# Queues that give each engine one piece of side work per half step in a four-layer attention and Fourier kernel

## The chip, the cores and the metric

The kernel runs on one core of one Trainium2 chip. The time is device microseconds of one launch, and the figure that counts is the median of several runs: 2229.14 us before the change (three runs: 2230.31, 2229.14 and 2216.46). The engines are TensorE (PE in the profile, PEld for its weight loads), VectorE (DVE), ScalarE (ACT), GpSimd (POOL) and SyncE (SP), which issues the transfers of this kernel in order.

## The reference

Four layers on an `x` of 2048 rows and 640 columns, all in float32: causal attention in a window of 256 rows with 32 heads of 20 columns, a Fourier mixing by matrices, and the same two again.

```python
def _A_ref(x, wqkv, wo):
    qkv = (x @ wqkv).reshape(B, S, 3, H, Dh).transpose(2, 0, 3, 1, 4)
    q, k, v = qkv[0], qkv[1], qkv[2]
    scores = einsum("bhqd,bhkd->bhqk", q, k) * (Dh ** -0.5)
    scores = where(0 <= i - j < 256, scores, -1e9)
    p = softmax(scores, axis=-1)
    return einsum("bhqk,bhkd->bhqd", p, v).transpose(0, 2, 1, 3).reshape(B, S, D) @ wo

def _B_ref(x, dft_seq_re, dft_seq_im, dft_hid_re, dft_hid_im):
    a = einsum("bsd,ed->bse", x, dft_hid_re)
    b = einsum("bsd,ed->bse", x, dft_hid_im)
    return einsum("ts,bse->bte", dft_seq_re, a) - einsum("ts,bse->bte", dft_seq_im, b)

x = x + _A_ref(_layernorm(x), A_wqkv, A_wo)
x = x + _B_ref(_layernorm(x), dft_seq_re, dft_seq_im, dft_hid_re, dft_hid_im)
x = x + _A_ref(_layernorm(x), A_wqkv, A_wo)
x = x + _B_ref(_layernorm(x), dft_seq_re, dft_seq_im, dft_hid_re, dft_hid_im)
```

## The kernel before

**Split operands.** Every large operand of a product is kept as two tiles: a leading part, which is the value rounded to the matmul's fp32r format, and a remainder, which is the value less its leading part. A product is three matmuls (leading by leading, leading by remainder, remainder by leading). So a tile that is to be multiplied is *cut*: one instruction writes the leading part (ACT, L180 in `split`, or a cast on POOL, L498) and one subtracts it from the value (L186 in `split`, on DVE or POOL, or L499 on POOL).

**The heads.** This is the middle part of each attention layer, and the change is almost all in it. The 32 heads are taken in 8 quads of 4, a quad in 16 steps of 128 rows: steps t = 0 to 127, 10 lead steps ahead of them, and two half steps (z = 0 and 1, two heads each) in each step. In a half step:

- PE makes the transposed scores of two heads for step t (`t_pair`, L595), the scores of two heads for step t + 10, of which only the row maxima are wanted (`s_head`, L567), and in the second half step the product of the probabilities with the values for step t - 1 (`pv`, L630, 24 matmuls).
- DVE adds the mask to each score tile and takes its row maximum (L572, two in a half step, each followed by a short read of the maximum). The bank is free when that is done.
- ACT takes the exponential (L605) and copies the product out (L637).
- POOL sets the probabilities outside the window to zero (L611 and L615, one pair in a half step). `pv` of a step needs them.

The three stages share a ring of six banks. A transposed score tile takes a bank that an L572 of the half step before has freed, so an L572 that is late makes the next half step's PE work late; masks that are late make `pv` late.

**Side work.** In the first half step PE also has a *fill*: matmuls of other work, taken in order from `more()`. In quads 0 to 5 these are the projections of later quads (`pieces`, L211, 64 rows by 512 columns). When a piece is complete its result is copied out by ACT (L497), cast by POOL one half step later (L498), subtracted by POOL one later (L499), and stored to memory four later (L500 and on, `store_qk`). Of its three buffers named `c`, the next piece but two takes the same one. The projection weights are cut as they come (`cut_chunk`, L186 on POOL, 384 and 256 columns). From t = 95 the fill is the output projection of the first three of five pieces of the heads' results, 16 tiles of 128 rows (`partials`); a tile is two fills of 18 matmuls of 320 columns, and DVE adds its two halves to `x` (L899). The remaining two pieces come after the heads (`late`).

**What a partial needs.** `load_o` loads a piece of the heads' results and the reciprocals of its row sums, multiplies them on POOL (L816, 8 half steps after the loads) and cuts the product (L186, POOL, 10 after). The output weights are cut too (`prepare`, L186, 640 columns on POOL; `poll_late`, L186 on DVE, in the same half step as the ACT part). `load_o` waits until its row sums are stored: it runs `tick` in a loop, and everything that is due in the skipped half steps is issued there and then. A row sum is loaded two half steps after its heads are done, its reciprocal (L650, DVE) is issued seven half steps after, and its store nine after (`finish`).

**Order.** `post(d, f)` runs `f` d half steps later; `tick` ends a half step and runs all that is due. Nothing limits how much one engine gets in a half step.

## Time and profile before

| what | us |
|---|---|
| median of three runs | 2229.14 |
| the profiled execution, its own time | 2223.97 |
| its span in the trace | 2222.2 |
| heads of the first attention layer, quads 0 to 7 | 161.72 to 543.98 |
| heads of the second attention layer | 1266.02 to 1644.50 |

The profile page gives for each group of instructions a line number, an engine, an operation and its tiles, then its busy time and the mean of one in ns, and the idle time just before it with what ended most of it. The window rows give the start and end of a stretch, its length, each engine's busy time with its number of instructions in brackets (PE, PEld, DVE, ACT, POOL), the clock that TensorE was granted (1.00 is full), the DMA share and GB/s. In a timeline row the first figure is the start, the second the length, and a bracket at its end says how long the engine had been idle and what ended that.

### The profile page before, as it was taken

To read this page: it belongs to the slowest core of one execution; us is meant where nothing else is said; L and a number is where in the kernel's file an instruction comes from. 1 tells how busy PE (TensorE), PEld (TensorE's weight loads), DVE (VectorE), ACT (ScalarE), POOL (GpSimd) and SP (SyncE) were. 2 spreads that over 40 slices of the span, in tenths; PEclk is the share of its full clock that TensorE was granted. 3 is DMA by queue.
4 is the path that set the end of the run, shared out by engine and by line. 5 is a ranking of instruction groups with operands and counts; after the bars stand their busy time and mean duration, and the time that the engine had idled before them with its cause. 6 is when DMAs were issued, how large, how long until landed. Compare 5 with 4: busy or idle time off the path is not lost.

```text
span 2222.2 us, 48837 instructions
## 1 busy us (share of the span) xinstructions
PE 2130.6 (96%) x17944; PEld 1782.5 (80%) x17944; DVE 1603.5 (72%) x3947; ACT 1128.9 (51%) x2101; POOL 1004.8 (45%) x1534
## 2 busy tenths in 40 slices
PE   7999999989989999999999999999989999999999
PEld 7887777677768888889999777776777688888899
DVE  6347788775897868785661578887758978687776
ACT  3116776656554545452441277776555545455432
POOL 3027777766614222332330476768665132332324
PEclk9999999999999999999999999999999999999999
DMA  5546656774535354656646466668754354546653
GB/s 184 171 148 187 195 182 204 221 205 142 181 125 184 120 183 141 211 182 199 209 145 185 153 184 192 192 200 232 201 168 148 118 186 142 170 138 220 218 163 129
DMA packets 220175, 392.10 MB, mean 176 GB/s; under 512 B 39200, under 2 KB 85792, under 8 KB 219936
## 3 DMA queue, kind: packets, MB, share of 16 engines
q1 hardware_dynamic: 219936, 388.98, 55.7%
q8 instruction: 142, 2.33, 0.4%
q14 instruction: 97, 0.79, 0.1%
HBM read 273.94 MB, written 113.77 MB: 174 GB/s over the span
## 4 chain that ended last, share of the span: by engine, by line
PE 71%; POOL 8%; DVE 8%; DMA 4%; issue 4%; ACT 4%; SPq 1%; POOLq 0%; ACTq 0%; DVEq 0%
PE banks L1280 27%; PE banks L193 14%; PE banks L211 10%; PE banks L630 6%; PE banks L1568 5%; PE banks L595 4%; PE banks L567 4%; POOL pt L611 2%; POOL pt L615 1%; POOL c L499 1%; POOL big L186 1%; ACT pt L605 1%; DVE qp L186 1%; DVE banks L572 1%; DMA vq<-v_d 1%
## 5 line engine op out<-in xcount | busy, mean ns | idle before, releaser
L572 DVE CUSTOM_DVE_ANT_0 banks<-banks,mask 128x384 f32<-128x384 f32 (+2 forms) x1024 | 528.0, 557 | 150.5 <-PE banks L567 127.9
L605 ACT ACTIVATE pt<-banks 128x768 f32<-128x768 f32 (+2 forms) x512 | 394.5, 772 | 165.8 <-PE banks L595 75.7
L611 POOL TENSOR_SCALAR_AFFINE_SELECT pt<-pt 128x256 f32<-128x256 f32 x512 | 210.5, 412 | 205.3 <-ACT pt L605 187.1
L211 PE MATMUL banks<-big,wc 64*128 64x512 f32 x1920 | 269.8, 395 | 0.4 <-DVE pt L396 0.4
L630 PE MATMUL banks<-pt,vq 128*32 128x128 f32 x5760 | 218.9, 279 | 12.1 <-POOL pt L611 12.1
L595 PE MATMUL banks<-qp,kp 61*128 61x384 f32 (+2 forms) x1024 | 208.2, 382 | 17.0 <-DVE mc L572 12.3
L567 PE MATMUL banks<-kp,qp 60*128 60x384 f32 (+2 forms) x1024 | 201.5, 347 | 12.9 <-DVE mc L572 10.8
L186 DVE TENSOR_TENSOR qp<-pt,qp 128x512 fp32r<-128x512 f32 (+1 forms) x209 | 178.7, 858 | 38.8 <-ACT qp L180 37.6
L211 PEld LDWEIGHTS banks<-big,wc 64*128 64x128 f32 x1920 | 185.1, 186 | 24.3 <-ACT x L497 1.8
L630 PEld LDWEIGHTS banks<-pt,vq 128*32 128x32 f32 x5760 | 145.0, 110 | 64.6 <-issue 37.0
L180 ACT ACTIVATE qp<-pt 128x512 fp32r<-128x512 f32 (+1 forms) x209 | 129.1, 624 | 118.6 <-DVE pt L1214 54.7
L615 POOL TENSOR_SCALAR_AFFINE_SELECT pt<-pt 128x256 f32<-128x256 f32 x448 | 184.6, 412 | 0.0
L595 PEld LDWEIGHTS banks<-qp,kp 61*128 61x128 f32 x1024 | 106.9, 186 | 81.2 <-DVE mc L572 52.0
L1280 PE MATMUL banks<-qp,big 128*128 128x512 f32 x630 | 153.4, 394 | 6.6 <-POOL big L186 3.9
L1213 POOL TENSOR_TENSOR pt<-pt,pt 128x512 f32<-128x512 f32 x34 | 50.6, 1489 | 240.3 <-DMA pt<-c 133.7
L567 PEld LDWEIGHTS banks<-kp,qp 60*128 60x128 f32 x1024 | 122.2, 188 | 36.7 <-DVE mc L572 22.5
L572 DVE DVE_READ_ACCUMULATOR2_ANT mc<- 128x1 f32 x1024 | 145.5, 142 | 0.0
L1280 PEld LDWEIGHTS banks<-qp,big 128*128 128x128 f32 x630 | 118.0, 189 | 32.9 <-POOL big L186 5.4
L180 ACT ACTIVATE c<-pt 128x512 fp32r<-128x512 f32 x144 | 88.2, 625 | 86.9 <-DVE pt L1214 41.1
L1280 PE MATMUL banks<-qp,xc 128*128 128x512 f32 x480 | 119.0, 391 | 6.8 <-DVE xc L186 4.2
L637 ACT ACTIVATE ou<-banks 128x128 f32<-128x128 f32 x256 | 71.5, 279 | 87.4 <-PE banks L630 76.7
L186 DVE TENSOR_TENSOR c<-pt,c 128x512 fp32r<-128x512 f32 x140 | 109.7, 789 | 8.4 <-ACT c L180 5.9
(241 smaller groups left out, 4469.8 us busy)
## 6 DMA issues: line engine op xcount, KB each, us to landing
pt<-c SPq DMA_DIRECT2D x188, 512.0 KB
qk_d<-c SPq DMA_DIRECT2D x80, 512.0 KB
kp<-qk_d SPq DMA_DIRECT2D x384, 80.0 KB
qp<-qk_d SPq DMA_DIRECT2D x384, 80.0 KB
kp<-u_d SPq DMA_DIRECT2D x32, 640.0 KB
o_d<-ou SPq DMA_DIRECT2D x64, 256.0 KB
x_d<-x SPq DMA_DIRECT2D x48, 320.0 KB
v_d<-pt SPq DMA_DIRECT2D x16, 768.0 KB
```

Of the source, the lines that this page charges most:

```text
L180: nc.scalar.activation(hi, src, AF.Copy, scale=-1.0 if neg else 1.0)
L186: (eng or nc.vector).tensor_tensor(out=lo, in0=src, in1=hi.bitcast(F32), op=OP.subtract)
L193: self.nc.tensor.matmul(p, x, y, start=n == 0, stop=n == last)
L211: self.nc.tensor.matmul(ps[a], x[r], y[r], start=half + i == 0, stop=half == 1 and i == n - 1, skip_group_check=True)
L567: nc.tensor.matmul(p, qp[quad % 2][b:b + 60, z, qb * P:(qb + 1) * P], kp[quad % 2][b:b + 60, z, k0 * P:(qb + 1) * P], start=True, stop=True)
L572: nc.vector.tensor_tensor_reduce(out=p, in0=p, in1=self.mask[:, 384 - n * P:], scale=1.0, scalar=NEG, op0=OP.add, op1=OP.max, accum_out=mc ...
L595: nc.tensor.matmul(self.banks[:, banks[e], :n * P], kp[quad % 2][b:b + 61, z, kb * P:(kb + 1) * P], qp[quad % 2][b:b + 61, z, kb * P:(kb + ...
L605: nc.scalar.activation(pt[quad, kb][:, 2 * z:2 * z + 2, :n * P], self.banks[:, b0:b1 + 1, :n * P], AF.Exp, scale=SCALE)
L611: nc.gpsimd.affine_select(out=t[:, :, 0:P], in_=t[:, :, 0:P], pattern=[[0, 2], [1, P]], compare_op=OP.is_ge, fill=0.0, base=0, channel_mul ...
L615: nc.gpsimd.affine_select(out=t[:, :, 256:384], in_=t[:, :, 256:384], pattern=[[0, 2], [-1, P]], compare_op=OP.is_gt, fill=0.0, base=0, ch ...
L630: nc.tensor.matmul(self.banks[32 * h:32 * h + 32, bank, :P], vq[:, 96 * (kb % 4) + 21 * h:96 * (kb % 4) + 21 * h + 32], t[:, h, (qb - kb) ...
L1280: nc.tensor.matmul(self.banks[:, bk, :], p, b[q], start=start and m == 0, stop=stop and last and m == 2, skip_group_check=True)
```

## The change

The change gives each of ACT, DVE and POOL a queue of pieces (`lanes`). `tick` still runs all that was posted, and then takes at most one piece from each queue. `job` puts a piece in a queue, `sub_job` a subtraction (in two halves if it is for POOL), `cut_job` a leading part for ACT which, when it runs, puts the subtraction in another queue; `flush` issues what is left under a name at once, and stands ahead of the uses.

- In `pieces` the cast stays on POOL; its subtraction goes to DVE half a step later, the store two after that.
- The weight cuts in `cut_chunk`, in `prepare` and in `poll_late` take ACT for the leading part and DVE, half a step later, for the remainder.
- `load_o` no longer waits by running `tick`; it posts itself again for the next half step. Its multiplication is two halves of 256 columns on POOL, one per half step. The cut's remainder is on POOL for the first piece, on DVE for the others.
- The reciprocal is issued 9 half steps after its heads are done, its store 11, and the store counts as done 2 half steps later.
- `more()` gives out no partial whose pieces aren't ready; a partial's sum is one addition of 640 columns (L970 of the new kernel) in place of two of 320.
- `pack`, which moves a quad's projected rows, waits for the stores of its rows.
- Two conditions more hold back steps of the Fourier layer that would overtake the late pieces, and a list of places there is in another order.

```diff
     def tick(self):
         self.slot += 1
         for k in sorted(k for k in self.posted if k <= self.slot):
             for f in self.posted.pop(k):
                 f()
+        for lane in self.lanes.values():
+            if lane and lane[0][0] <= self.slot:
+                lane.popleft()[2]()
+
+    def job(self, lane, key, fn):
+        if self.slot is None or self.after:
+            fn()
+        else:
+            self.lanes[lane].append((self.slot + 1, key, fn))
...
+    def sub_job(self, lane, key, lo, src, hi, done=None):
+        eng = {"dve": self.nc.vector, "pool": self.nc.gpsimd}[lane]
+        n = 2 if lane == "pool" else 1
+        w = src.shape[-1] // n
+        for i in range(n):
+            c = slice(i * w, (i + 1) * w)
+            def sub(c=c, last=i == n - 1):
+                eng.tensor_tensor(out=lo[..., c], in0=src[..., c], in1=hi[..., c].bitcast(F32), op=OP.subtract)
+                if last and done:
+                    done()
+            self.job(lane, key, sub)
+
+    def cut_job(self, lane, key, hi, lo, src, done=None):
+        def first():
+            self.nc.scalar.activation(hi, src, AF.Copy)
+            self.sub_job(lane, key, lo, src, hi, done)
+        self.job("act", key, first)
...
-            for i, ks in enumerate((slice(0, 3), slice(3, KC))):
-                self.post(3 * i, lambda ks=ks: self.split(w[:, 0, ks], w[:, 1, ks], raw[:, ks], eng=self.nc.gpsimd))
+            for ks in (slice(0, 3), slice(3, KC)):
+                self.cut_job("dve", ("w", c), w[:, 0, ks], w[:, 1, ks], raw[:, ks])
...
             self.nc.scalar.activation(r, p, AF.Copy)
-            self.post(1, lambda: self.nc.gpsimd.tensor_copy(st[:, 0, :], r))
-            self.post(2, lambda: self.nc.gpsimd.tensor_tensor(
-                out=st[:, 1, :], in0=r, in1=st[:, 0, :].bitcast(F32), op=OP.subtract))
-            self.post(6, lambda: self.store_qk(c, sb, st))
+            def cast():
+                self.nc.gpsimd.tensor_copy(st[:, 0, :], r)
+                self.sub_job("dve", ("qk", c, sb), st[:, 1, :], r, st[:, 0, :],
+                             lambda: self.post(2, store))
...
+            self.job("pool", ("qk", c, sb), cast)
...
-            at = (2, 7, 9) if quad < NQ - 1 else (1, 5, 6)
+            at = (2, 9, 11) if quad < NQ - 1 else (1, 5, 6)
...
-                self.stored.add((quad, bk))
+                self.post(2 if quad < NQ - 1 else 0, lambda: self.stored.add((quad, bk)))
...
-            if not made[0] and self.early_o[0]["left"]:
+            if not self.left and not self.ready_part():
                 return None
...
+        if not self.after and not all((q, sb) in self.stored for q in range(h0 // 4, h1 // 4)):
+            def again():
+                o["left"] -= 1
+                self.load_o(o, sb, k, raw, rr)
+            self.post(1, again)
+            return
...
-        self.post(8, lambda: nc.gpsimd.tensor_tensor(out=raw, in0=raw, in1=rr, op=OP.mult))
-        self.post(10, cut)
+        def parts():
+            hi, lo = o[k]
+            self.cut_job("pool" if k == 0 else "dve", key, hi, lo, raw, lambda: self.post(0 if k < EARLY else 3, done))
+        def half(i):
+            cs = slice(i * 256, (i + 1) * 256)
+            nc.gpsimd.tensor_tensor(out=raw[:, cs], in0=raw[:, cs], in1=rr[:, cs], op=OP.mult)
+            if i:
+                parts()
+        for i in range(2):
+            self.post(7, lambda i=i: self.job("pool", key, lambda: half(i)))
...
-            next(self.early_l[2])
-            for i in range(2):
-                self.defer(2 + 2 * i, lambda i=i: next(self.early_l[i]))
+            for k in (2, 0, 1):
+                self.cut_job("dve", "ew", *self.early_w[k], self.early_raw[k])
...
-            for hf in range(2):
-                cs = slice(hf * 320, (hf + 1) * 320)
-                nc.vector.tensor_tensor(out=y[:, cs], in0=ps[hf], in1=y[:, cs], op=OP.add)
+            nc.vector.tensor_tensor(out=y, in0=self.banks[:, b0:b0 + 2, :320], in1=y, op=OP.add)
...
-            self.split(hi[:, cs], lo[:, cs], r[:, cs])
+            self.cut_job("dve", "lw", hi[:, cs], lo[:, cs], r[:, cs])
...
+        if any(n >= at and (len(self.late_o) <= sb or self.late_o[sb]["left"]) for sb, at in ((2, 4), (3, 7))):
+            return False
```

On POOL in quad 0, at steps 3 to 5, stood these rows before; `c` is a projected piece, `wc` a weight, `pt_94` to `pt_97` are the probabilities of four successive steps.

```order
L498 CAST c<-x 128x512
L611 AFFINE_SELECT pt_97<-pt_97 128x2x128
L615 AFFINE_SELECT pt_97<-pt_97 128x2x128
L499 TENSOR_TENSOR c<-x,c 128x512
L498 CAST c<-x 128x512
L611 AFFINE_SELECT pt_94<-pt_94 128x2x128
L615 AFFINE_SELECT pt_94<-pt_94 128x2x128
L186 TENSOR_TENSOR wc<-x,wc 128x384
L499 TENSOR_TENSOR c<-x,c 128x512
L611 AFFINE_SELECT pt_94<-pt_94 128x2x128
L615 AFFINE_SELECT pt_94<-pt_94 128x2x128
```

At the same place stand now:

```order
L543 CAST c<-x 128x512
L666 AFFINE_SELECT pt_97<-pt_97 128x2x128
L670 AFFINE_SELECT pt_97<-pt_97 128x2x128
L543 CAST c<-x 128x512
L666 AFFINE_SELECT pt_94<-pt_94 128x2x128
L670 AFFINE_SELECT pt_94<-pt_94 128x2x128
L666 AFFINE_SELECT pt_94<-pt_94 128x2x128
L670 AFFINE_SELECT pt_94<-pt_94 128x2x128
```

All subtractions have left this stretch; two casts are all that is left between the masks (L666 and L670 are the old L611 and L615).

On DVE in quad 1, at steps 3 and 4, stood nothing before but mask additions (`ISA banks,mc<-banks,mask`) with their reads, and a reciprocal ahead of these steps.

```order
L572 ISA banks,mc<-banks,mask 128x384
L572 ISA mc 128x1
L572 ISA banks,mc<-banks,mask 128x384
L572 ISA mc 128x1
L650 RECIPROCAL rc<-sm 128x16
L572 ISA banks,mc<-banks,mask 128x384
L572 ISA mc 128x1
```

There stand now, one or two between each pair of mask additions (L627 is the old L572, L207 the new subtraction):

```order
L207 TENSOR_TENSOR c<-x,c 128x512
L627 ISA banks,mc<-banks,mask 128x384
L627 ISA mc 128x1
L627 ISA banks,mc<-banks,mask 128x384
L627 ISA mc 128x1
L207 TENSOR_TENSOR c<-x,c 128x512
L627 ISA banks,mc<-banks,mask 128x384
L627 ISA mc 128x1
L627 ISA banks,mc<-banks,mask 128x384
L627 ISA mc 128x1
L705 RECIPROCAL rc<-sm 128x16
L207 TENSOR_TENSOR wc<-x,wc 128x384
```

The subtraction of the other 256 columns of `wc` follows behind the next pair. The four subtractions of this stretch come in four half steps on end, and two more of `c` come at steps 11 and 12 of the same quad.

On PE at the first partial, the end of quad 5, stood before (L630 is `pv`, L211 with `big` tiles the partial):

```order
L630 MATMUL banks<-pt_97,vq_92 32x128 x4
L630 MATMUL banks<-pt_94,vq_93 32x128 x4
L630 MATMUL banks<-pt_95,vq_93 32x128 x4
L595 MATMUL banks<-qp_104,kp_103 128x128 x2
L567 MATMUL banks<-kp_560,qp_105 128x384 x2
L211 MATMUL banks<-big_5456,big_5459 128x320 x18
L595 MATMUL banks<-qp_104,kp_103 128x128 x2
L567 MATMUL banks<-kp_560,qp_105 128x384 x2
```

From the same half step on stand now, up to the first partial (L650, L622, L685 and L253 are the old L595, L567, L630 and L211):

```order
L650 MATMUL banks<-qp_105,kp_560 128x384 x2
L622 MATMUL banks<-kp_560,qp_105 128x384 x2
L650 MATMUL banks<-qp_105,kp_560 128x384 x2
L622 MATMUL banks<-kp_560,qp_105 128x384 x2
L685 MATMUL banks<-pt_95,vq_93 32x128 x4
L685 MATMUL banks<-pt_96,vq_93 32x128 x4
L685 MATMUL banks<-pt_97,vq_93 32x128 x4
L650 MATMUL banks<-qp_105,kp_560 128x384 x2
L622 MATMUL banks<-kp_560,qp_105 128x384 x2
L253 MATMUL banks<-big_5455,big_5456 128x320 x18
```

The first partial has moved from t = 95 to t = 97, into quad 6, so that five steps (92 to 96) have no fill where three had none; the last of the 16 partials then has no steps left and follows the heads as 18 matmuls of full height.

51 lines of the change are left out of this document (40 added, 11 removed).

## The prediction

> **What bounds the kernel.** I read the page first, for the engines and the waits:
>
> ```profile
> PE 2130.6 (96%) x17944; PEld 1782.5 (80%) x17944; DVE 1603.5 (72%) x3947; ACT 1128.9 (51%) x2101; POOL 1004.8 (45%) x1534
> L572 DVE CUSTOM_DVE_ANT_0 banks<-banks,mask 128x384 f32<-128x384 f32 (+2 forms) x1024 | 528.0, 557 | 150.5 <-PE banks L567 127.9
> L611 POOL TENSOR_SCALAR_AFFINE_SELECT pt<-pt 128x256 f32<-128x256 f32 x512 | 210.5, 412 | 205.3 <-ACT pt L605 187.1
> ```
>
> PE is the bound over the whole span, and POOL is idle half of it; so a gain can only lie where PE stands still. For that I read the windows by quad of the heads: a quiet quad, the first quads of both layers, and then the stretches inside quads where half steps are long.
>
> ```profile
> 161.72:209.81 48.09, 44.41 (x590) 33.15 (x588) 35.88 (x137) 31.22 (x56) 34.50 (x73) 0.96 0.64 201
> 209.81:253.76 43.95, 43.03 (x616) 32.57 (x612) 35.34 (x135) 31.73 (x58) 31.55 (x70) 1.00 0.61 183
> 1266.02:1314.31 48.29, 44.52 (x590) 33.02 (x588) 35.87 (x137) 31.30 (x56) 34.51 (x73) 0.96 0.64 205
> ...
> 164.82:172.53 7.71, 5.46 (x38) 3.96 (x40) 3.88 (x14) 2.81 (x5) 6.75 (x13) 0.78 0.73 242
> 212.44:216.46 4.02, 3.66 (x42) 2.88 (x39) 3.46 (x13) 2.91 (x6) 2.30 (x6) 1.00 0.70 196
> 218.84:226.73 7.89, 7.33 (x112) 5.14 (x108) 6.44 (x25) 6.28 (x12) 7.63 (x14) 1.00 0.43 127
> 234.31:235.56 1.25, 1.25 (x24) 0.98 (x18) 1.02 (x5) 0.97 (x3) 0.77 (x2) 1.00 0.44 136
> ```
>
> The quiet quad (209.81) takes 43.95, and both first quads some 4 more. The row at 234.31 is one quiet second half step: 1.25, PE busy all of it, DVE 1.02. Three quiet half steps (first, second, first) are 4.02, so a quiet first one is (4.02 - 1.25) / 2 = 1.385. In the second half step PE has no slack and DVE has 0.23.
>
> **The start of a layer's heads.** The three half steps at 164.82 are the same as those at 212.44 and take 7.71 in place of 4.02: 3.69 more. The timeline has the cause.
>
> ```profile
> 165.20 0.62 POOL L498 CAST c<-x 128x512 fp32r<-128x512 f32 x1 [6.45 <-DMA qk_d<-c]
> 165.78 2.51 POOL L499 TENSOR_TENSOR c<-x,c 128x512 fp32r<-128x512 f32 x2
> 168.25 0.41 POOL L611 TENSOR_SCALAR_AFFINE_SELECT pt<-pt 128x256 f32<-128x256 f32 x1
> ...
> 168.72 0.41 PE L630 MATMUL banks<-pt,vq 128*32 128x128 f32 x4 [1.95 <-POOL pt L611]
> ```
>
> POOL waits for a store out of a `c` buffer, then does a cast and two subtractions, and the first mask of the quad stands behind them; PE waits for that mask. In the new order the eight casts of the lead steps stand together on POOL, without subtractions, and each store follows its subtraction by two half steps. So the 3.13 of POOL work go (0.62 stays somewhere), and the store comes earlier. What is next late is DVE, which gets eight subtractions in the lead steps, where PE is busy with projections: I give back 0.5. Gain 3.2 in each of two layers: **-6.4**.
>
> **Bursts in quads 0 to 4.** The window 218.84 holds five half steps, 3.1 to 5.1. Quiet they would take 3 x 1.25 + 2 x 1.385 = 6.52; they take 7.89, 1.37 more, most of it where `pv` waits for a mask behind POOL's subtractions:
>
> ```profile
> 223.68 1.03 POOL L186 TENSOR_TENSOR wc<-x,wc 128x384 fp32r<-128x384 f32 x1
> 224.66 1.30 POOL L499 TENSOR_TENSOR c<-x,c 128x512 fp32r<-128x512 f32 x1
> ...
> 226.38 0.41 PE L630 MATMUL banks<-pt,vq 128*32 128x128 f32 x4 [0.56 <-POOL pt L611]
> ```
>
> That stall goes with the subtractions. What comes is on DVE, where no such subtraction stands in these quads before; I take it from other places.
>
> ```profile
> 453.10 0.25 DVE L650 RECIPROCAL rc<-sm 128x16 f32<-128x16 f32 x1 [3.12 <-DMA sm<-ou]
> 453.27 0.54 DVE L572 CUSTOM_DVE_ANT_0 banks<-banks,mask 128x384 f32<-128x384 f32 x1
> 453.73 0.60 DVE L572 CUSTOM_DVE_ANT_0 banks<-banks,mask 128x384 f32<-128x384 f32 x1
> 454.25 0.88 DVE L899 TENSOR_TENSOR big<-banks,big 128x320 f32<-128x320 f32 x2
> ...
> 561.39 0.68 DVE L1200 TENSOR_TENSOR vq<-pt 128x512 f32<-128x512 f32 x1
> 561.99 0.68 DVE L186 TENSOR_TENSOR qp<-pt,qp 128x512 fp32r<-128x512 f32 x1
> ```
>
> Start to start, two mask additions take 0.98 to 1.03 and 512 columns 0.60; 384 and 256 I scale to 0.45 and 0.30, a reciprocal is 0.17. The four half steps 3.1 to 5.0 then hold 4 x 1.02 + 2 x 0.60 + 0.45 + 0.30 + 0.17 = 6.20 of DVE work against 5.27 of quiet time: 0.93 over, in place of 1.37. At steps 11 and 12 two half steps get 2 x 1.02 + 1.20 = 3.24 against 2.64: 0.6 over, of which some 0.4 is there already behind POOL's subtractions. Per quad -0.4 + 0.2 = -0.2. The other end is what a DVE subtraction costs beside POOL:
>
> ```profile
> 508.52 1.11 DVE L186 TENSOR_TENSOR qp<-cr,qp 128x320 fp32r<-128x320 f32 x1 [1.29 <-ACT qp L180]
> 513.06 0.73 DVE L186 TENSOR_TENSOR qp<-cr,qp 128x320 fp32r<-128x320 f32 x1 [0.59 <-ACT qp L180]
> 516.35 0.49 DVE L186 TENSOR_TENSOR qp<-cr,qp 128x320 fp32r<-128x320 f32 x1 [0.36 <-ACT qp L180]
> ...
> 507.98 2.79 POOL L186 TENSOR_TENSOR big<-x,big 128x512 fp32r<-128x512 f32 x2
> ...
> 513.04 0.40 POOL L615 TENSOR_SCALAR_AFFINE_SELECT pt<-pt 128x256 f32<-128x256 f32 x1
> ```
>
> The same operation takes 0.49 with POOL idle, 0.73 started beside a mask (0.24 more) and 1.11 beside two subtractions (0.62 more). With 0.24 on each of six the quad comes to -0.2 + 1.4 = +1.2. I take the middle, +0.5, for ten quads: **+5**, ends -2 and +12.
>
> [...]
>
> **Quad 5.** The stretch from t = 92 on:
>
> ```profile
> 419.78:436.32 16.54, 13.81 (x151) 9.75 (x147) 9.35 (x35) 7.42 (x17) 13.37 (x22) 0.69 0.80 244
> 1524.23:1529.67 5.44, 4.91 (x68) 3.24 (x64) 5.00 (x18) 3.94 (x8) 5.44 (x11) 1.00 0.68 164
> 1524.23:1539.08 14.85, 11.95 (x151) 8.75 (x147) 9.55 (x35) 7.64 (x17) 13.29 (x22) 0.89 0.83 257
> ...
> 425.18 2.50 POOL L816 TENSOR_TENSOR x<-x,rr 128x512 f32<-128x512 f32 x2
> ```
>
> Four steps take 16.54 and 14.85. Two multiplications in a row hold up POOL's masks for 2.50, and two cuts follow. Two steps without fill and without these take 5.44, so four take 10.88: gains of 5.66 and 3.97, **-9.6**. It includes that the partial at t = 95 is gone from here. The halves on POOL, one per half step, leave room: masks 0.77 and a half of some 0.63 are 1.40, about a half step.
>
> **Quads 6 and 7.** Four reciprocals wait on DVE for their row sums, with the mask additions queued behind them and PE waiting for these. One is at 453.10 above; the others:
>
> ```profile
> 481.27 0.25 DVE L650 RECIPROCAL rc<-sm 128x16 f32<-128x16 f32 x1 [1.33 <-DMA sm<-ou]
> 1554.07 0.25 DVE L650 RECIPROCAL rc<-sm 128x16 f32<-128x16 f32 x1 [1.18 <-DMA o_d<-ou]
> 1581.22 0.25 DVE L650 RECIPROCAL rc<-sm 128x16 f32<-128x16 f32 x1 [1.59 <-DMA sm<-ou]
> ...
> 508.45:512.00 3.55, 1.59 (x32) 0.83 (x28) 3.48 (x10) 1.72 (x4) 3.55 (x4) 1.00 0.02 5
> 1608.54:1612.10 3.56, 1.58 (x34) 0.84 (x30) 3.49 (x10) 1.72 (x4) 3.56 (x4) 1.00 0.02 7
> ```
>
> The waits add up to 7.2. Two half steps more (some 3 us here) cover them all; but five subtractions of 512 columns come to DVE in quad 6, beside partial sums, and I take **-5**, ends -7 and -2. In quad 7 one half step takes 3.55 in both layers, POOL busy all through it with two cuts of 2.79 and a multiplication, DVE with a cut beside them; quiet it is 1.25. With halves, and the late weights' remainder half a step behind ACT, I leave 0.3 of the 2.3: **-4.0**.
>
> **The end of the heads.** The last partial moves behind them, 18 matmuls of full height:
>
> ```profile
> 542.02 2.03 PE L193 MATMUL banks<-qp,kp 128*128 128x320 f32 x12
> ```
>
> Twelve take 2.03, so 18 some 3.0, with nothing beside them: **+6.0** in two layers. The Fourier edits issue nothing new, at zero; a held-back step would cost PE idle time that shows as a wait for a remainder.
>
> **The sum.** -6.4 + 5 - 9.6 - 5 - 4 + 6.0 = -14.0. The profiled execution took 2223.97, which gives 2210.0. The median of the runs is 2229.14, 5.2 above it, which gives 2215.1. I take 2212 for the median. Within 1% (22 us, about what a measurement here can tell from no change) of 2229 reaches from 2207 to 2251.
>
> **Rivals.**
> - *The bursts are free.* Bursts -2, quad 6 -7, quad 7 -4.6, and the last partial hides beside the end of the heads: -6.4 - 2 - 9.6 - 7 - 4.6 = -29.6, some 2197. For it: DVE's idle time in L572's row, 150.5. Against it: in a half step of 1.25 with 1.02 on DVE it is only 0.23. Chance 0.18.
> - *VectorE becomes the bound (slower).* Some 60 remainders in quads 0 to 4 and 40 in quads 5 to 7, each of which meets POOL work and takes 0.62 more, as at 508.52, all of it on PE's path: with bursts at -2 instead of 5 and 62 more, -21 + 62 = +41, some 2267. It decides from a mean of about 1.0 for 512 columns. Against it: POOL has lost the long subtractions, and masks alone cost 0.24. Chance 0.10.
> - *It is given back.* 0.24 for each of the 100: -21 + 24 = +3, some 2230; a longer stretch without fill helps this, since PE's granted clock was 0.69 in the stretch at 419.78. Chance 0.22.
> - *It doesn't do what it says:* the queues are flushed in clumps and the stalls come back, 2224 to 2229. The order of the instructions speaks against it. Chance 0.05.
>
> My forecast has 0.45. [...]
>
> **Numbers.** Faster by over 1%: all of the first rival and 0.10 of my forecast's lower end, 0.28. Slower by over 1%: the second rival, 0.10. Within: 0.62. The range of 2190 to 2240 leaves out the second rival and a little of each end of the others.
>
> **What would show it.** Right: the first quads as long as the second; no PE wait for a mask in quads 1 to 4, half steps 3.1 to 5.0 of about 1.5 each; no reciprocal that waits; 18 matmuls behind the heads. Wrong: 512-column subtractions on DVE with a mean over 0.9, masks or `pv` that wait for something new, quads 1 to 4 over 45, or a wait in the Fourier layers that wasn't there.

## The result and the profile after

The changed kernel takes 2224.77 us (median of 12 runs, 2220.75 to 2226.25); the kernel before, in 12 runs, 2223.1 us. The ratio is 0.9996 with a 95% interval of 0.9981 to 1.001: no change that can be told from none. The time lies inside the predicted range of 2190 to 2240, but the gain of some 14 us isn't there. Both profiled executions are close together: a span of 2222.2 before, 2219.0 after. All of this difference is there before the first heads begin (at 161.72 before, at 158.38 after), while the first loads come in. It is scatter: the profiles of ten kernels with the changed kernel's code up to there reach this point 0.6 us earlier to 5.9 us later than the changed kernel's own. So the question is where the expected gain went.

The page of the changed kernel, the same lines as before (L627 is the old L572, L666 the old L611):

```profile
PE 2131.4 (96%) x17908; PEld 1786.0 (80%) x17908; DVE 1669.5 (75%) x4031; ACT 1126.6 (51%) x2101; POOL 910.6 (41%) x1456
L627 DVE CUSTOM_DVE_ANT_0 banks<-banks,mask 128x384 f32<-128x384 f32 (+2 forms) x1024 | 526.8, 556 | 98.5 <-PE banks L622 80.5
L666 POOL TENSOR_SCALAR_AFFINE_SELECT pt<-pt 128x256 f32<-128x256 f32 x512 | 215.8, 422 | 282.0 <-ACT pt L660 243.2
```

94 us of work have left POOL, 66 have come to DVE, and PE is as busy as before. DVE's idle time ahead of the mask additions has fallen from 150.5 to 98.5: its slack went, without a shorter kernel.

The windows by quad of the changed kernel, first quads 0 and 1, then quads 5 to 7 of the first layer, then quads 0 and 5 to 7 of the second (start and end, length, busy time of PE, PEld, DVE, ACT and POOL, TensorE's granted clock, DMA share, GB/s):

```profile
158.38:203.39 45.01, 43.34 (x590) 32.38 (x588) 38.96 (x144) 31.10 (x56) 27.23 (x64) 1.00 0.61 198
203.39:247.94 44.55, 42.99 (x616) 32.60 (x612) 38.49 (x141) 31.73 (x58) 26.94 (x64) 1.00 0.60 189
...
382.22:430.96 48.74, 45.03 (x586) 32.02 (x582) 40.47 (x143) 33.61 (x61) 32.77 (x72) 0.89 0.73 224
430.96:486.43 55.47, 51.36 (x766) 42.25 (x763) 44.22 (x150) 32.48 (x60) 34.81 (x75) 0.94 0.76 198
486.43:534.78 48.35, 44.60 (x705) 36.70 (x705) 28.35 (x80) 32.17 (x58) 35.23 (x73) 1.00 0.51 155
...
1259.90:1304.89 44.99, 43.37 (x590) 32.36 (x588) 38.95 (x144) 31.11 (x56) 27.23 (x64) 1.00 0.62 197
...
1483.59:1528.86 45.27, 41.83 (x588) 30.20 (x584) 40.02 (x142) 33.42 (x61) 32.77 (x72) 1.00 0.69 201
1528.86:1587.08 58.22, 52.13 (x768) 42.44 (x764) 44.55 (x152) 32.61 (x60) 34.76 (x75) 0.94 0.82 215
1587.08:1635.47 48.39, 44.62 (x703) 36.74 (x703) 28.34 (x80) 32.16 (x58) 35.22 (x73) 1.00 0.55 164
```

The same quads 5 to 7 of the kernel before, first layer and second:

```profile
385.37:436.32 50.95, 46.96 (x604) 34.22 (x600) 35.66 (x135) 33.77 (x62) 41.60 (x77) 0.90 0.75 217
436.32:493.47 57.15, 51.48 (x784) 42.76 (x781) 42.76 (x157) 32.53 (x58) 37.63 (x72) 0.97 0.76 204
493.47:543.98 50.51, 45.95 (x710) 37.44 (x707) 25.60 (x83) 31.98 (x58) 35.19 (x69) 1.00 0.53 163
...
1489.81:1539.08 49.27, 44.87 (x604) 33.18 (x600) 35.84 (x135) 33.99 (x62) 41.51 (x77) 0.97 0.76 228
1539.08:1593.43 54.35, 50.35 (x785) 41.34 (x781) 42.75 (x157) 32.51 (x58) 37.52 (x72) 1.00 0.77 209
1593.43:1644.50 51.07, 46.32 (x711) 37.42 (x707) 25.62 (x83) 31.98 (x58) 35.18 (x69) 1.00 0.52 161
```

Against the terms of the sum (after less before, both layers; the end of the heads is how much later the same matmul of the Fourier layer comes, counted from the end of quad 7, once both kernels run evenly, from the 400th on):

| place | forecast | measured |
|---|---|---|
| quads 0, start and burst | -6.4 and +1 | 45.01 - 48.09 and 44.99 - 48.29: -6.4 |
| quads 1 to 4, bursts | +4 | 0.5 to 1.1 each, +6.5 in eight |
| quads 5 | -9.6 | -2.2 and -4.0: -6.2 |
| quads 6 | -5 | -1.7 and +3.9: +2.2 |
| quads 7 | -4.0 | -2.16 and -2.68: -4.8 |
| ends of the heads | +6.0 | +3.8 and some +5.9: +9.7 |

These sum to some +1, in line with no change. The starts and quads 7 came as forecast or better. Against the forecast, quads 6 are 7.2 us worse, the ends 3.7, quads 5 3.4 and the bursts of quads 1 to 4 2.5.

**Bursts.** Five half steps (from the second half of step 3 to the second half of step 5) of quad 1 in the changed kernel, a DVE and a POOL row beside each other at step 4, PE behind them, and the group of all such DVE rows in quads 1 to 4 (count, busy time, mean in ns):

```profile
212.41:220.33 7.92, 7.18 (x112) 4.98 (x108) 7.91 (x28) 6.51 (x13) 6.09 (x13) 1.00 0.62 199
...
215.84 0.82 DVE L207 TENSOR_TENSOR c<-x,c 128x512 fp32r<-128x512 f32 x1
...
216.07 0.85 POOL L670 TENSOR_SCALAR_AFFINE_SELECT pt<-pt 128x256 f32<-128x256 f32 x1
...
217.24 0.45 PE L650 MATMUL banks<-qp,kp 61*128 61x384 f32 x2 [0.46 <-DVE mc L627]
...
L207 DVE TENSOR_TENSOR c<-x,c 128x512 fp32r<-128x512 f32 x16 | 13.5, 841 | 0.1
```

7.92 where it was 7.89 before: one stall has taken the place of another of the same size. DVE is now busy through all of it (7.91), and PE waits for the mask additions where it used to wait for masks: in quads 1 to 4 of the first layer its waits for masks, 2.3 us before, are gone, and its waits for mask additions rose from 0.7 to 5.9. In steps 11 and 12, where two more remainders meet the mask additions, the four half steps take 5.99 in place of 5.46. A remainder of 512 columns takes 0.82 beside a mask (the mean of 16 is 0.84, where 0.68 had been seen alone), and the mask beside it 0.85 in place of 0.41: beside each other both took longer.

**The end of the heads.** PE, POOL and DVE of the changed kernel behind the first layer's heads (L235 are the late tiles' matmuls, L1070 their additions, L885 and L207 the multiplication and remainder of pieces of `load_o`):

```profile
542.43 3.22 PE L235 MATMUL banks<-qp,kp 128*128 128x320 f32 x18 [0.51 <-DVE x L1070]
549.23 1.15 PE L235 MATMUL banks<-qp,kp 128*128 128x320 f32 x6 [3.59 <-DVE x L1070]
...
544.60 2.79 POOL L885 TENSOR_TENSOR cr<-cr,rr 128x256 f32<-128x256 f32 x4
...
546.72 2.06 DVE L207 TENSOR_TENSOR kp<-cr,kp 128x512 fp32r<-128x512 f32 x2 [2.11 <-ACT kp L215]
548.69 0.49 DVE L1070 TENSOR_TENSOR x<-banks,big 128x320 f32<-128x320 f32 x1
```

`job` issues a piece at once when the heads are over (`self.after`). So four half multiplications, two leading parts and two remainders come in one clump, and a late tile's addition, for which PE waits 3.59, stands behind them on DVE. The second layer has the same wait, 3.59 again. (The last partial itself cost what was forecast: its 18 matmuls run in two groups of nine, 1.5 us each, one group still in the last half step of quad 7.)

**Quad 5.** The four steps without fill, 92 to 95, of the changed kernel, first layer and second:

```profile
416.43:430.96 14.53, 12.25 (x133) 7.58 (x129) 10.83 (x37) 6.56 (x15) 8.28 (x18) 0.64 0.87 271
1517.78:1528.86 11.08, 9.03 (x135) 5.73 (x131) 10.39 (x36) 6.41 (x15) 8.29 (x18) 1.00 0.77 204
```

The forecast was 10.88 for each. The second layer has it. The first does the same work at a granted clock of 0.64 and takes 3.45 more: the clock is 0.5 there for 17.07 us from 420.59 on (10.24 before).

**Quad 6.** DVE, PE and SyncE of the changed kernel from 1523 us on, at steps 93 to 97 of the second layer (L944 loads x for the first partials, 320 KB each; L702 loads the row sums of four heads; `mt` are row maxima that are added to the projected rows; SPq is the issue of a transfer):

```profile
1535.36 0.25 DVE L705 RECIPROCAL rc<-sm 128x16 f32<-128x16 f32 x1 [3.12 <-DMA sm<-ou]
...
1536.18 0.44 PE L622 MATMUL banks<-kp,qp 60*128 60x384 f32 x2 [2.28 <-DMA qp<-mt]
...
1523.27 1.79 SPq L944 DMA_DIRECT2D big<-x_d  x4
...
1525.58 1.64 SPq L585 DMA_DIRECT2D qp<-qk_d  x3
...
1529.92 0.61 SPq L702 DMA_DIRECT2D sm<-ou  x1
...
1529.92:1533.34 3.42, 3.14 (x46) 2.52 (x48) 2.33 (x9) 2.36 (x4) 2.00 (x5) 1.00 1.01 382
```

This is the one reciprocal of the heads that still waits notably, but it waits as long as the longest before. The row sums were asked for at 1529.92 and used at 1535.36, 5.44 later; for the first 3.42 of that the DMA engines were full (share 1.01). In the first layer no transfer is waited for here: steps 94 and 95, at half clock, take 7.66 where the second layer takes 5.08, and the transfers come in time.

### The profile page after: what moved, and what is told of

Same layout as the page of the kernel before. It is cut to its first block, busy times and chain, and to the rows that moved or that the text cites. A ratio compares the mean times of both kernels' runs of the same rounds, so it can differ in the third digit from the quotient of the medians.

```text
span 2219.0 us, 49084 instructions
## 1 busy us (share of the span) xinstructions
PE 2131.4 (96%) x17908; PEld 1786.0 (80%) x17908; DVE 1669.5 (75%) x4031; ACT 1126.6 (51%) x2101; POOL 910.6 (41%) x1456
## 3 DMA queue, kind: packets, MB, share of 16 engines
q8 instruction: 141, 2.31, 0.5%
## 4 chain that ended last, share of the span: by engine, by line
PE 70%; DVE 13%; issue 6%; DMA 4%; ACT 3%; POOL 3%; SPq 0%; ACTq 0%; DVEq 0%; POOLq 0%
PE banks L1360 28%; PE banks L235 13%; PE banks L253 9%; PE banks L685 5%; PE banks L650 5%; DVE banks L627 5%; PE banks L1648 4%; PE banks L622 4%; DMA qp<-qk_d 1%; DVE c L207 1%; POOL big L228 1%; DVE mc L627 1%; DMA qk_d<-c 1%; DVE qp L228 1%; PE banks L337 1%
## 5 line engine op out<-in xcount | busy, mean ns | idle before, releaser
L627 DVE CUSTOM_DVE_ANT_0 banks<-banks,mask 128x384 f32<-128x384 f32 (+2 forms) x1024 | 526.8, 556 | 98.5 <-PE banks L622 80.5
L666 POOL TENSOR_SCALAR_AFFINE_SELECT pt<-pt 128x256 f32<-128x256 f32 x512 | 215.8, 422 | 282.0 <-ACT pt L660 243.2
L253 PE MATMUL banks<-big,wc 64*128 64x512 f32 x1920 | 271.2, 394 | 0.4 <-DVE pt L438 0.4
L650 PE MATMUL banks<-qp,kp 61*128 61x384 f32 (+2 forms) x1024 | 211.8, 383 | 32.5 <-DVE mc L627 28.5
L685 PE MATMUL banks<-pt,vq 128*32 128x128 f32 x5760 | 213.4, 280 | 1.5 <-ACT pt L660 1.5
L622 PE MATMUL banks<-kp,qp 60*128 60x384 f32 (+2 forms) x1024 | 204.9, 352 | 6.6 <-DVE mc L627 4.1
L670 POOL TENSOR_SCALAR_AFFINE_SELECT pt<-pt 128x256 f32<-128x256 f32 x448 | 207.2, 462 | 0.0
L253 PEld LDWEIGHTS banks<-big,wc 64*128 64x128 f32 x1920 | 186.5, 185 | 22.9 <-ACT x L540 1.7
L650 PEld LDWEIGHTS banks<-qp,kp 61*128 61x128 f32 x1024 | 108.6, 186 | 100.4 <-DVE mc L627 76.5
L685 PEld LDWEIGHTS banks<-pt,vq 128*32 128x32 f32 x5760 | 143.4, 110 | 49.5 <-issue 36.4
L222 ACT ACTIVATE c<-pt 128x512 fp32r<-128x512 f32 x150 | 93.6, 626 | 160.3 <-POOL pt L1280 52.9
L222 ACT ACTIVATE qp<-pt 128x512 fp32r<-128x512 f32 (+1 forms) x195 | 119.9, 624 | 105.3 <-DVE pt L1294 54.0
L228 DVE TENSOR_TENSOR c<-pt,c 128x512 fp32r<-128x512 f32 x150 | 123.0, 822 | 52.0 <-ACT c L222 49.9
L228 DVE TENSOR_TENSOR qp<-pt,qp 128x512 fp32r<-128x512 f32 (+1 forms) x191 | 151.2, 799 | 11.7 <-ACT qp L222 9.0
L1360 PE MATMUL banks<-qp,big 128*128 128x512 f32 x630 | 152.4, 394 | 2.9 <-POOL qp L228 1.7
L622 PEld LDWEIGHTS banks<-kp,qp 60*128 60x128 f32 x1024 | 119.9, 188 | 32.1 <-DVE mc L627 19.5
L627 DVE DVE_READ_ACCUMULATOR2_ANT mc<- 128x1 f32 x1024 | 144.3, 141 | 0.0
L1360 PEld LDWEIGHTS banks<-qp,big 128*128 128x128 f32 x630 | 119.0, 190 | 28.8 <-POOL qp L228 2.3
L1360 PE MATMUL banks<-qp,xc 128*128 128x512 f32 x480 | 117.2, 390 | 0.7 <-DVE xc L228 0.7
L543 POOL CAST c<-x 128x512 fp32r<-128x512 f32 x64 | 40.3, 633 | 181.3 <-ACT x L540 180.3
```

What stands on the lines that cost most here:

```text
L222: nc.scalar.activation(hi, src, AF.Copy, scale=-1.0 if neg else 1.0)
L228: (eng or nc.vector).tensor_tensor(out=lo, in0=src, in1=hi.bitcast(F32), op=OP.subtract)
L253: self.nc.tensor.matmul(ps[a], x[r], y[r], start=half + i == 0, stop=half == 1 and i == n - 1, skip_group_check=True)
L622: nc.tensor.matmul(p, qp[quad % 2][b:b + 60, z, qb * P:(qb + 1) * P], kp[quad % 2][b:b + 60, z, k0 * P:(qb + 1) * P], start=True, stop=True)
L627: nc.vector.tensor_tensor_reduce(out=p, in0=p, in1=self.mask[:, 384 - n * P:], scale=1.0, scalar=NEG, op0=OP.add, op1=OP.max, accum_out=mc ...
L650: nc.tensor.matmul(self.banks[:, banks[e], :n * P], kp[quad % 2][b:b + 61, z, kb * P:(kb + 1) * P], qp[quad % 2][b:b + 61, z, kb * P:(kb + ...
```

## The experiments

The theory after this reading: the gain at the starts and in quads 7 is real, and is given back (1) by VectorE's remainders in the bursts, (2) by the clump behind the heads, and (3) near the end of quad 5, where the stretch without fill makes PE slow or the transfers late. Eleven kernels were run, in groups that share runs of the kernel before. The changed kernel's 2224.77 is of an earlier group. The kernel before has medians of 2221.13 to 2224.23 in these groups, so some 3 us of a difference between kernels of two groups can be the group's. The medians, in us:

| kernel | median | kernel before, same group | ratio, 95% interval |
|---|---|---|---|
| a_pool | 2206.19 | 2224.23 | 0.9917, 0.9901 to 0.9934 |
| a_dummy | 2223.27 | 2224.23 | 0.9999, 0.9989 to 1.0008 |
| a_queue | 2215.88 | 2224.23 | 0.9962, 0.9948 to 0.9977 |
| a_recip | 2222.12 | 2224.23 | 0.9991, 0.9979 to 1.0003 |
| a_loads | 2226.51 | 2221.13 | 1.0018, 1.0005 to 1.0031 |
| b_pieces | 2223.77 | 2221.13 | 1.001, 0.9997 to 1.0022 |
| c_pool_queue | 2200.24 | 2221.13 | 0.9904, 0.9886 to 0.9922 |
| c_all | 2197.14 | 2221.13 | 0.9887, 0.987 to 0.9903 |
| c_small | 2198.35 | 2222.05 | 0.9893, 0.9869 to 0.9918 |
| c_extra | 2205.62 | 2222.05 | 0.9938, 0.992 to 0.9955 |
| c_both | 2194.17 | 2222.8 | 0.9883, 0.9858 to 0.9907 |

### Remainders of quads 0 to 5 on GpSimd (a_pool)

```diff
-                self.sub_job("dve", ("qk", c, sb), st[:, 1, :], r, st[:, 0, :],
+                self.sub_job("dve" if self.lead else "pool", ("qk", c, sb), st[:, 1, :], r, st[:, 0, :],
...
-                self.cut_job("dve", ("w", c), w[:, 0, ks], w[:, 1, ks], raw[:, ks])
+                self.cut_job("dve" if self.lead else "pool", ("w", c), w[:, 0, ks], w[:, 1, ks], raw[:, ks])
```

> The changed kernel, but the remainders of the projected pieces and of their weights in quads 0 to 5 go to GpSimd again, in two halves, one per half step. Theory (the new half steps of 1.99 and 1.69 in each quad are VectorE's remainders): quads 1 to 4 fall from 44.6-44.9 us to 42.5-43.2, the time falls by 12 to 20 us against the changed kernel. Rival (these half steps have another cause, or the masks now wait behind GpSimd's halves as they did before): quads 1 to 4 stay at 43.9 or above, the time within 4 us of the changed kernel.

18.6 us less than the changed kernel. Its windows of quad 1 and of the same five half steps:

```profile
204.96:247.88 42.92, 42.56 (x616) 32.66 (x612) 35.34 (x135) 31.60 (x58) 32.51 (x76) 1.00 0.63 203
...
214.00:220.93 6.93, 6.93 (x110) 5.05 (x106) 6.00 (x24) 6.14 (x12) 6.64 (x15) 1.00 0.51 159
```

6.93 where 7.92 stood, PE busy all of it. Quad 1 takes 42.92, 1.63 less than with the remainders on DVE and 1.03 less than before the change. In the profiles quads 0 to 4 of both layers lose 15.7 us together, as the theory said, and quads 5 another 5.4, where the long half clock of the first layer is gone too (both quads take 44.30). So what the queues have to offer is there: GpSimd's work in halves, one per half step, hid beside the masks here. Putting the remainders on VectorE cost more than it saved, although GpSimd was the engine whose stalls could be seen before. The run changes the engine and the size of the pieces at once; halves on VectorE, one per half step, weren't tried.

### Matmuls that keep TensorE busy (a_dummy)

```diff
+                if r is None and k == 0 and not self.left and self.part_t == 0 and not self.lead:
+                    x = self.early_w[0][0]
+                    ps = [self.bank("m") for _ in range(2)]
+                    for i in range(8):
+                        c = slice(64 * (i % 2), 64 * (i % 2) + 64)
+                        nc.tensor.matmul(ps[i % 2], x[c, :P], x[c, P:], start=True, stop=True, skip_group_check=True)
```

> The changed kernel with 8 more matmuls (64 rows by 512, result unused) in each first half step that has no fill, steps 92 to 96. Theory (PE is so lightly used there that its clock is halved, and the half clock sets the length): the half clock near the end of quad 5 (17.07 us long in the first layer) goes, steps 92 to 96 take about 13.1 us in place of 18.3 and 14.0, the time falls by 4 to 9 us. Rival (the loop of scores, VectorE and ScalarE sets these steps, and the clock only follows): they take as long or up to 5 us longer per layer, the time rises by 0 to 10 us.

The long half clock went (one stretch of 3.41 us is left there), and steps 92 to 96 of the first layer fell from 18.3 to 14.5 us, near what the theory said (in the second layer, at full clock before, they took 14.0 and now 14.5). Steps 92 to 95 of the first layer:

```profile
419.24:430.77 11.53, 11.09 (x165) 8.49 (x161) 10.37 (x36) 6.70 (x15) 8.05 (x18) 1.00 0.81 234
```

The time didn't fall clearly: the wait for row sums, absent from the first layer of the changed kernel, appeared there:

```profile
437.09 0.25 DVE L705 RECIPROCAL rc<-sm 128x16 f32<-128x16 f32 x1 [2.92 <-DMA sm<-ou]
```

The half clock sets the length of these steps in the first layer, but behind it stand the transfers, and they take back most of what a faster PE gains: quad 5 of the first layer takes 45.78 in place of 48.74, quad 6 57.77 in place of 55.47. Both of the expectations missed the total, -1.5 us.

### The queues kept behind the heads (a_queue)

```diff
-        if self.slot is None or self.after:
+        if self.slot is None:
             fn()
```

> The changed kernel, but pieces stay in their queues behind the heads too, where the changed kernel issues them all at once. Theory (the stall of 3.59 us behind the heads comes from four multiplications on GpSimd and two remainders on VectorE that are issued in one clump ahead of a late tile's addition): the stall goes, 2.5 to 3.5 us per attention layer, 5 to 7 in all. Rival (the late tile waits for these pieces anyway): the stall moves by under 1 us and the time stays within 2 us.

8.9 us less than the changed kernel in the medians, somewhat more than expected. The chain behind the heads of the first layer:

```profile
543.81 4.12 PE L235 MATMUL banks<-qp,kp 128*128 128x320 f32 x24 [0.51 <-DVE x L1070]
547.76 2.23 PE L1360 MATMUL banks<-qp,big 128*128 128x512 f32 x9
```

The wait of 3.59 is gone, and the Fourier layer's first matmuls (L1360) come at 547.76, where they came at 554.35 in the changed kernel. Not all of this lasts: from the 400th of these matmuls on, counted from the end of quad 7, 3.9 us are left in the first layer and 2.4 in the second, 6.3 together, which is within the theory's 5 to 7.

### Reciprocals as early as before (a_recip)

```diff
-            at = (2, 9, 11) if quad < NQ - 1 else (1, 5, 6)
+            at = (2, 7, 9) if quad < NQ - 1 else (1, 5, 6)
...
-                self.post(2 if quad < NQ - 1 else 0, lambda: self.stored.add((quad, bk)))
+                self.stored.add((quad, bk))
```

> The changed kernel with the reciprocals issued 7 half steps after their heads and counted as stored at their store (9), as before the change. Theory (the first partial then comes at step 95 again, the stretch without fill is three steps and no partial is left behind the heads): the ends of both layers' heads lose 6 us, the stretch some 4 more, and VectorE's waits for row sums cost up to 7 again: 0 to 10 us less than the changed kernel. Rival (the later reciprocals are what the gain of the last quads comes from): waits of 1 to 3 us return in four places and the time rises by 3 to 7 us.

2.7 us less in the medians, and the interval overlaps that of the changed kernel: neither view is told apart. The first partial is at step 95 again and none is left behind the heads (which shortened the ends), but steps 88 to 112 take 84.2 and 85.0 us in place of 81.3 and 80.6, and eight reciprocals wait again for over 0.5, 11.9 us in sum. The two roughly cancel.

### The loads of x spread (a_loads)

```diff
-            self.load_y(range(AHEAD_X))
+            for i in range(AHEAD_X):
+                self.defer(1 + 2 * i, lambda i=i: self.load_y([i]))
```

> The changed kernel with the four loads of x for the first partials (320 KB each, issued in a row at step 91) issued one in two steps, at 92 to 98. Theory (they fill the DMA engines when the row sums of the last half of quad 5 are to be loaded, and VectorE's reciprocal and PE wait for that): in the second layer the waits of 3.12 and 2.28 us at steps 97 and 98 go and these two steps fall from some 11 to some 6 us; in the first layer little changes, since the half clock gives the transfers time; 3 to 6 us less. Rival (the projections' stores and the loads of quad 7 fill the engines as well): the waits stay over 1.5 us and the time within 2 us.

The waits at steps 97 and 98 of the second layer went, as the theory said. But two half steps of 4.82 and 2.68 us appeared at steps 101 and 102, with waits of 2.31 for row sums and 1.77 for row maxima; quad 6 took the same time (58.25), and the kernel 1.7 us more than the changed kernel. The theory of four bunched loads was too narrow.

### One edit in the kernel before (b_pieces)

```diff
-            self.post(2, lambda: self.nc.gpsimd.tensor_tensor(
+            self.post(2, lambda: self.nc.vector.tensor_tensor(
                 out=st[:, 1, :], in0=r, in1=st[:, 0, :].bitcast(F32), op=OP.subtract))
-            self.post(6, lambda: self.store_qk(c, sb, st))
+            self.post(4, lambda: self.store_qk(c, sb, st))
```

> The kernel before, with one edit: the subtraction of a projected piece goes to VectorE, two half steps after the copy, and the store two after it. Theory (the late masks at the start of a layer's heads are GpSimd's two subtractions behind a late store): the first quads fall by 3 us each, to about 45; quads 1 to 4 keep GpSimd's weight cuts and get two VectorE remainders at steps 3 and 11, and stay at 43.9 to 44.9; the time falls by 0 to 7 us. Rival (the start's gain comes from the queues, one piece per half step): the first quads stay at 48.

The first quads take 44.89 and 45.95 in place of 48: the start's gain comes from this edit alone, without any queue. Which of its two halves brings it, the engine or the earlier store, isn't told apart. Quads 1 take 44.06 and 44.21. The whole isn't faster than before. In its profile steps 88 to 112 took 80.9 and 83.0, where they took 84.9 and 80.4 before; that doesn't explain the median, and where the start's gain went is open.

### Both mends, and the transfers (c_pool_queue, c_all, c_small, c_extra, c_both)

c_pool_queue is the edits of a_pool and a_queue together; c_all adds that of a_loads. c_small is c_pool_queue with the rows of quad 7 loaded in part: it leaves out most of two of the three copies of quad 7's projected rows, and what quad 5 left stands in their place. c_both is the same with the spread loads. These two measure what the bytes cost; they don't do the whole computation. c_extra is c_pool_queue with `load_y(range(2 * AHEAD_X))`.

```diff
+                    cl = slice(sb * 512, sb * 512 + 64) if part and quad == NQ - 1 else cols
-                    src = self.qk[l, r0:r0 + 40, cols].rearrange("(z r) s -> r z s", z=2)
+                    src = self.qk[l, r0:r0 + 40, cl].rearrange("(z r) s -> r z s", z=2)
-                    todo.append(lambda d=dst[b:b + 20, :, cols], src=src: put(d, src))
+                    todo.append(lambda d=dst[b:b + 20, :, cl], src=src: put(d, src))
```

> The remainders on GpSimd in halves and the queues kept behind the heads, together, in the changed kernel. If the two causes are apart, their gains against the changed kernel (18.6 and 8.9 us) add up: 2195 to 2201 us. If both stood for the same time: 2204 to 2208.

2200.24: within the range for two separate causes, some 3 us short of the full sum. In the profiles steps 88 to 112 of both layers take 3.0 more than in a_pool.

> The same with the four loads of x spread over steps 92 to 98. Here both layers run the stretch without fill at full clock and wait for row sums at steps 97 and 98 (3.65 and 3.25 us in the first layer). Theory (the loads fill the DMA engines): both go, 8 to 11 us less than without the spreading, 2186 to 2192. Rival (other transfers): within 3 us.

2197.14, 3.1 less, and the intervals of the two overlap. Waits for row sums and maxima were left at steps 97 to 102, spread over more places.

> The kernel with the remainders on GpSimd in halves and the queues kept behind the heads, in which quad 7's projected rows are loaded in part: of the second and third of the three copies only 64 of 512 columns (the rest is what quad 5 left there), with the same number of transfers in the same order. That takes some 2 MB of transfers out of steps 91 to 108. Theory (the bytes that the DMA engines have to move there set when row sums and row maxima arrive): steps 88 to 112 fall from 79.5-81.2 us to under 77 in both layers, and the waits for row sums and maxima at steps 97 to 102 fall under 1 us; the time falls by 4 to 10 us. Rival (the order and number of transfers in SyncE's queue set it): within 2 us.

> The same kernel with all of quad 7's rows and four more loads of x (320 KB each, loaded again later) in a row at step 91. Theory (bytes): 1.3 MB more at some 300 GB/s, 3 to 5 us more per layer in steps 88 to 112, 6 to 10 us in all. Rival (order and number): the four issues take 2 us of SyncE's queue, 0 to 3 us in all.

> Both at once: the four loads of x spread over steps 92 to 98, and quad 7's rows loaded in part (of the second and third copies 64 of 512 columns), with GpSimd's halves and the queues behind the heads. With the spreading alone the wait moved from step 97 to step 101; with the smaller loads alone it stayed at step 97, behind the four loads in a row. Theory (bytes in front of a row sum): no wait for a row sum or for maxima over 0.7 us is left, steps 88 to 112 take 75 to 77 us in both layers in place of 79.5 to 81.5. Rival (something else, such as the row sums' own latency): waits of over 1.5 us stay, and over 78.5 us.

Steps 88 to 112 of both layers, for the kernel before, the changed kernel, c_pool_queue, c_all, c_small, c_extra and c_both, in this order:

```profile
408.57:493.47 84.90, 76.50 (x1090) 60.88 (x1087) 60.85 (x221) 49.02 (x90) 61.15 (x113) 0.92 0.78 211
1513.02:1593.43 80.41, 73.51 (x1091) 58.43 (x1087) 61.04 (x221) 49.23 (x90) 60.97 (x113) 0.98 0.79 216
```

```profile
405.13:486.43 81.30, 74.92 (x1054) 58.26 (x1051) 64.38 (x219) 48.18 (x90) 53.94 (x115) 0.90 0.76 208
1506.50:1587.08 80.58, 72.45 (x1056) 56.63 (x1052) 64.27 (x219) 48.12 (x90) 53.90 (x115) 0.96 0.79 213
```

```profile
399.50:480.69 81.19, 72.05 (x1054) 56.85 (x1050) 62.94 (x217) 48.05 (x90) 55.70 (x119) 0.96 0.78 218
1490.06:1569.53 79.47, 71.42 (x1056) 55.85 (x1052) 62.99 (x217) 48.03 (x90) 55.64 (x119) 0.98 0.75 218
```

```profile
399.95:479.71 79.76, 71.43 (x1054) 56.03 (x1050) 63.02 (x217) 48.12 (x90) 55.57 (x119) 0.98 0.78 211
1491.35:1572.88 81.53, 72.62 (x1054) 57.55 (x1050) 62.88 (x217) 48.13 (x90) 55.64 (x119) 0.96 0.79 210
```

```profile
402.81:482.24 79.43, 71.47 (x1054) 56.12 (x1050) 63.04 (x217) 48.04 (x90) 55.72 (x119) 0.98 0.65 194
1491.52:1567.63 76.11, 69.99 (x1054) 54.84 (x1050) 63.06 (x217) 48.22 (x90) 55.71 (x119) 1.00 0.66 196
```

```profile
399.03:481.29 82.26, 71.73 (x1056) 56.45 (x1052) 63.06 (x217) 48.24 (x90) 55.74 (x119) 0.96 0.80 219
1489.79:1573.91 84.12, 71.79 (x1054) 56.38 (x1051) 63.06 (x217) 48.16 (x90) 55.68 (x119) 0.96 0.81 216
```

```profile
396.35:471.47 75.12, 69.47 (x1055) 54.71 (x1052) 63.15 (x217) 48.01 (x90) 55.57 (x119) 1.00 0.68 198
1479.18:1555.69 76.51, 69.73 (x1054) 54.80 (x1050) 63.09 (x217) 48.05 (x90) 55.51 (x119) 1.00 0.66 200
```

The first four of these kernels move the same bytes and take 79.5 to 81.5 here, but for the first layer of the kernel before, whatever POOL and DVE do; the DMA engines are 0.75 to 0.79 busy on average and full in the bursts (1.01 in the changed kernel's 3.42 us from 1529.92 on). (Over all ten kernels with these bytes it was 78.8 to 85.0, with the most where the first partial came early, in a_recip.) More loads ahead of a row sum make it longer: in c_extra the reciprocal waits 4.62 and 5.86 us, where in c_pool_queue it was 3.66 and 2.23; this kernel adds bytes and transfers at once. (Its expectation took some 300 GB/s; 281 were measured in the changed kernel from 1523 to 1535 us.) Fewer bytes alone help the second layer (76.11), and hardly the first, where the wait stays at 3.00, since the four loads of x are still in front. With both the stretch takes 75.12 and 76.51, where the spreading alone (c_all) took 79.76 and 81.53; one wait of over 0.7 is left, 1.46 for row maxima in the second layer. The number and the order of the transfers are the same in c_small as in c_pool_queue, and in c_both as in c_all, so it is the bytes, and how they are bunched ahead of small loads that are needed soon. Each kernel was profiled once, and c_both's profile is of the shortest of its runs (2188.57), c_all's of the longest of its own (2202.51), so the size of the gain is uncertain: c_small's median is only 1.9 under that of c_pool_queue, c_both's 3.0 under that of c_all. What speaks against scatter is that three of the four stretches with fewer bytes are shorter than each of the twenty with all of them (78.8 at least).

The version to keep is c_all, or c_pool_queue, which is simpler: 1.1% and 1.0% faster than before with the whole computation done.

## Why the prediction was wrong

- *The start of a layer's heads.* Right: -6.4 for two quads 0 (-5.4 with their bursts was forecast), and b_pieces shows that the remainder's place and the earlier store bring it, without a queue.
- *The bursts.* The size was near (forecast +0.5 per quad, some +0.8 measured), by the reason given: DVE's work in four half steps, with remainders that meet masks. What the forecast didn't ask is what the same work costs on POOL when it is spread, and so it took the loss as the price of the queues. a_pool shows that it is the price of whole remainders on VectorE: in the first of these stretches 7.92 on DVE, and 6.93 in halves on POOL.
- *Quads 6: the step that failed most.* "Two half steps more (some 3 us here) cover them all": -5 was forecast, +2.2 came. The step took the reciprocals' waits away by time alone and didn't ask what the row sums wait for. In its place the runs show that transfers bound steps 97 to 102: the row sums took 5.44 us from issue to use, behind loads that filled the DMA engines (share 1.01). A wait that went at one step came back at another (2.92 in a_dummy, 2.31 and 1.77 in a_loads), unless bytes went (c_both, 75.12 and 76.51 in place of 79.76 and 81.53). The prediction's own rows had signs of it: a DMA share of 0.80 and 0.83 in the stretch just before, and row sums as what was waited for.
- *Quads 5.* "Four steps take 16.54 and 14.85 ... so four take 10.88" was right for the second layer (11.08) and failed in the first (14.53), where the sum had no term for the clock: PE ran at 0.64 of it. The third rival had named that. a_dummy shows it: at full clock the same four steps take 11.53. -9.6 was forecast for quads 5, -6.2 came.
- *Quads 7.* Right, -4.8 for -4.0.
- *The end of the heads.* The partial was forecast (+6.0); the clump of pieces behind it wasn't (+9.7 measured). It was seen as a rival, "the queues are flushed in clumps", for the whole kernel with 0.05, and the diff has the line that does it, `self.slot is None or self.after`. What decides there isn't the order of the instructions in the heads but what `job` does once they are over; a_queue took 8.9 off the median by that line, 6.3 of it seen behind the heads.
- *The rivals.* "It is given back" comes nearest in its number, but by transfers, the clump and the clock as well as by slower remainders. "VectorE becomes the bound" named the right engine for the bursts with too high a price: 0.62 more was never reached (the longest of its L207 rows on DVE is 1.24), 0.16 was the mean (0.84 against 0.68).
- *The base.* The three runs before had a median of 2229.14, 12 runs have 2223.1; 6 us of the forecast's distance were never there.

## What to carry to other kernels

When side work moves between engines, compare three places for it, not two: where it was, where it goes, and where it was but in smaller pieces; the stall that can be seen on the old engine may come from the size of a piece and not from the engine. Ahead of counting a wait as a gain, see what the stretch needs of transfers: here, with a DMA share of 0.76 to 0.79 and a wait for a small load behind large ones, taking time out of the compute engines moved the wait (a_dummy: 2.92 in the first layer, which had none). Where matmuls are taken out of a stretch, look at the granted clock too (0.64 here, and 3.45 us more than at 1.00). And read what a scheduler does in its other modes (here: behind the heads), since a queue that is bypassed at one place gives back there what it gained elsewhere.

## What was not expected of the hardware

TensorE's granted clock fell while PE was far from idle. In the 3.42 us before it halved, in the first layer of the changed kernel, PE was busy for 2.46, 0.72 of the time, by the profile (in the second layer for 1.13 of 3.41), with no wait over 0.5 us in the first; and at half clock it was busy for 3.12 of 3.41 without the clock coming back at once (it stayed at 0.50 to 437.66):

```profile
417.17:420.59 3.42, 2.46 (x34) 1.45 (x33) 3.33 (x12) 1.89 (x5) 3.08 (x6) 1.00 0.59 178
420.59:424.00 3.41, 3.12 (x32) 2.03 (x32) 2.19 (x8) 1.61 (x4) 1.49 (x4) 0.50 0.93 261
1533.34:1536.75 3.41, 1.13 (x18) 0.61 (x14) 1.39 (x7) 0.81 (x1) 1.47 (x4) 1.00 0.54 178
```

In the profiles of the kernel before and of the changed kernel every stretch at half clock is a multiple of 3.41 us long: six of 3.41, three of 6.83, one of 10.24 and one of 17.07 (but for the last of each, at the end of the trace: 3.74 and 1.64). In the first layer the stretch without fill, in which no wait of PE is over 0.53 us, came with 17.07 us at half clock, and with eight more matmuls a step (a_dummy) only 3.41 us of half clock were left. The same work ran at full clock in the second layer until 1536.75, so the length of the stretch at half clock isn't set by the work alone. What sets when the clock falls and when it comes back, these runs don't show.
